# Layer norm scalars of a two-block mixer: three small GpSimd operations in one, against four operations planned apart

## The chip, the cores and the metric

The kernel runs on one core of one Trainium2 chip. The metric is the device time of one execution in microseconds (us). A core has five instruction streams that run beside each other and wait for each other by semaphores: PE (TensorE, the matmuls; its weight loads are listed as PEld), DVE (VectorE), ACT (ScalarE), POOL (GpSimd) and SP (SyncE, which only issues transfers here). Each executes its own instructions strictly in order.

## The reference

The input x is 2048 rows of 512 features. Four stages follow each other: mixer A, mixer B, mixer A, mixer B, each on the layer norm of x and added to x. The layer norm is what the change is about:

```python
def _layernorm(x, axis=-1, eps=1e-5):
    m = jnp.mean(x, axis=axis, keepdims=True)
    v = jnp.var(x, axis=axis, keepdims=True)
    return (x - m) / jnp.sqrt(v + eps)
# A: qkv = x @ wqkv; 32 heads of 16, each position attends to itself and to the
#    positions 2, 4, .. 14 before it; softmax; the result @ wo
# B: h = gelu(layernorm(x) @ w1), its four quarters of features shifted by +1, -1, +2, -2
#    rows, @ w2, added to x: x1;  then x1 + gelu(layernorm(x1) @ w3) @ w4, w3 to 1792 features
x = A_x
x = x + _A_ref(_layernorm(x, axis=-1), A_wqkv, A_wo)
x = x + _B_ref(_layernorm(x, axis=-1), B_w1, B_w2, B_w3, B_w4)
# ... and both once more with the same weights
```

## The kernel before

The rows are cut into four blocks of 512, and a block into four tiles of 128 rows (one row per partition). Layer l = 0, 1 and block b = 0 .. 3 make eight units n = 4 l + b. For each unit there are five stages, whose names stand in the texts below:

- p1: layer norm of x, transposed, times wqkv; q, k and v go out to DRAM (`p1_quarters` for the unit 0, `p1_stream` for the others);
- p2: the attention, on DVE: a product of 128x4096 elements, a sum over it, softmax, a second product and three additions, four times per unit (`p2_unit`);
- p3: the attention's result times wo, added to x, layer norm, transposed, times w1, gelu, into h;
- p4: the shifted h times w2, added to the layer norm's value, layer norm again, transposed;
- p5: times w3, gelu, times w4, over 14 chunks of 128 features, added to x. In unit 0 it works on the weights in f32 as they are; for the other units they are split before into a high and a low f16 half by `big_pair`. Most matmuls take three passes over such halves.

A layer norm of one tile runs so: the sum of the row comes from the instruction that made x; `sq_dev` is an ACT Square with bias and an accumulated sum (the variance, unscaled); `power` makes the two scalars per row from these sums; `normed` applies them to the 128x512 tile on ACT, POOL or DVE; then come transposes on PE and copies into f16 halves. `power` is the place of the change. It is called 84 times: for the four tiles of unit 0's p1, for the 16 tiles of p1 in layer 1 (units 4 to 7), for 32 tiles in p3 and for 32 in p4. Its scalars are columns of small tiles named a (p1), b (p3) and c (p4), with a number for the role: a_0 is the sum, a_1 the squares' sum, a_2 the variance with epsilon (`ve`), a_3 the power (`r`), a_4 the shift (`nb`); in b these are b_0, b_1, b_2, b_3 and b_6. `powers` does the same for four columns at once and stays as it is.

Nothing is scheduled while the program runs. Every operation is entered in a graph with its reads and writes and with the engines on which it could run. Two tables then decide: ORDER lists all operations as 4 x its number + the choice of the engine, and this order is kept on each engine; SLOTS gives each logical buffer its place among the buffers of its kind (mm and acc in PSUM; x, w, f, g, nT, h, kv, prod and so on in SBUF). A list of buffers shared in this way means that an operation can wait for a slot too.

All instructions are issued through one wrapper, so the profile gives them all one line, L282 before (L295 after), and they are told apart by the names of their tiles.

Of the kernel before, what the change touches and what calls it, by code (L numbers as in the profile page):

```python
# [268 lines left out]
def tile_mixer(ctx, tc, x_d, wqkv_d, wo_d, w1_d, w2_d, w3_d, w4_d, out_d):  # L269
# [243 lines left out]
    def sq_dev(key, src, tot, ss, i, r, k=None):  # L513

        s, k = slice(i, i + 1), i if k is None else k
        act(key, lambda: A.activation(junk, src(), AF.Square, bias=tot.t[:, k:k + 1], scale=-float(D),
                                      accum_out=ss.t[:, s]), r + [(tot, k)], [(ss, i)])

    def power(key, ss, ve, r, i, c1, c2, tot, c, nb, k=None, j=None):

        s, k, j = slice(i, i + 1), i if k is None else k, i if j is None else j
# [748 lines left out]
```

## Time and profile before

| | |
|---|---|
| runs before (median; lowest, highest) | 1188.43 us (1188.41, 1188.98) |
| the profiled execution, its own time | 1188.87 us |
| its span, first to last instruction | 1187.0 us |
| mean granted clock of TensorE | 0.99 |
| PE busy | 1144.8 us, 96% |
| DVE, ACT, POOL busy | 919.9, 581.8, 389.5 us |
| main DMA queue | 60.3% of 16 engines' span |

A row of the profile by groups gives the engine and operation, what it writes and reads (buffer numbers left out), the shape, how often, then the busy time in us and the mean of one in ns. A row of the timeline starts with the start and the duration in us, and in brackets stands the idle time before it and what ended it. Rows of stages have the window, its length and, for each engine in turn, its busy time and number of instructions.

### The profile page before, as it was taken

Reading aid. Unit: us, or ns where it says so; the run is one execution under the profiler, and the core shown is the slowest. Engines: PE = TensorE matmul, PEld = TensorE weight load, DVE = VectorE, ACT = ScalarE, POOL = GpSimd, SP = SyncE. Lnnn points to the kernel's source line nnn. Section 1 sums busy time; section 2 is a strip of 40 time slices with the busy share of each in tenths; the row PEclk is TensorE's granted clock in tenths of the full one; section 3 lists DMA queues with packets and bytes.
Section 4 is the critical chain, followed back from the end, with each engine's and each line's share of the span. In section 5 each row is a group of like instructions: output and inputs, shape, how many; then the busy total and the mean of one; then the engine's idle time right before and its main releaser. Section 6 shows DMA issues by size and latency. Waiting matters only on the chain.

```text
span 1187.0 us, 15150 instructions
## 1 busy us (share of the span) xinstructions
PE 1144.8 (96%) x5334; PEld 545.3 (46%) x5334; DVE 919.9 (77%) x992; ACT 581.8 (49%) x1044; POOL 389.5 (33%) x486
## 2 busy tenths in 40 slices
PE   9699999999898999999999999999999999999998
PEld 6444444554343444444444444444444444444454
DVE  6989999999987898599965988889848998224122
ACT  7584465333777454353453546465435463342231
POOL 4320021021556514341752345531516153315000
PEclk9999999899999999999999999999999999999999
DMA  6975664557698645965476786884388546414221
GB/s 217 313 259 174 198 195 142 166 168 183 197 310 244 181 121 124 267 192 145 106 194 211 197 183 159 226 199 148 99 201 256 155 114 197 108 62 112 90 92 62
DMA packets 240533, 206.80 MB, mean 174 GB/s; under 512 B 107276, under 2 KB 167940, under 8 KB 240456
## 3 DMA queue, kind: packets, MB, share of 16 engines
q1 hardware_dynamic: 238784, 204.01, 60.3%
q10 hardware_dynamic: 1672, 1.82, 0.5%
q8 instruction: 42, 0.69, 0.2%
q14 instruction: 35, 0.29, 0.1%
HBM read 141.03 MB, written 39.47 MB: 152 GB/s over the span
## 4 chain that ended last, share of the span: by engine, by line
PE 86%; ACT 5%; DMA 4%; DVE 3%; issue 1%; SPq 1%; POOL 0%; ACTq 0%; DVEq 0%
PE mm L282 60%; PE acc L282 26%; DMA w<-in_A_x_dram 1%; DMA w<-in_B_w_dram 1%; ACT junk L282 1%; ACT g L282 1%; SPq L282 1%; DVE L L282 1%; DVE prod L282 1%; DMA xt<-g 1%; DMA kv<-kv 1%; ACT f L282 1%; ACT ev L282 1%; DVE g L282 0%; POOL g L282 0%
## 5 line engine op out<-in xcount | busy, mean ns | idle before, releaser
L282 PE MATMUL mm<-nT,w 128*128 128x512 f16 (+1 forms) x1288 | 306.7, 391 | 5.2 <-DMA w<-w 4.5
L282 PE MATMUL acc<-w,g 128*128 128x512 f16 (+1 forms) x1260 | 307.3, 393 | 1.7 <-POOL g L282 1.7
L282 ACT ACTIVATE mm<-mm,s_w 128x512 f32<-128x512 f32 (+1 forms) x144 | 90.8, 631 | 254.3 <-PE mm L282 254.1
L282 POOL TENSOR_TENSOR g<-f,g 128x512 f16<-128x512 f32 x80 | 121.6, 1528 | 244.8 <-ACT g L282 149.5
L282 PE MATMUL mm<-wq_hl,xt 128*128 128x512 f16 x864 | 196.5, 380 | 3.4 <-ACT ev L282 1.8
L282 PEld LDWEIGHTS <-w 128*128 128x128 f16 x1344 | 124.9, 98 | 146.3 <-issue 5.0
L282 PEld LDWEIGHTS <-g 128*128 128x128 f16 x1272 | 124.3, 98 | 147.5 <-POOL g L282 2.2
L282 PEld LDWEIGHTS <-xt 128*128 128x128 f16 x1008 | 98.6, 98 | 121.8 <-issue 4.6
L282 DVE TENSOR_TENSOR prod<-kv,L 128x4096 f32<-128x4096 f32 x32 | 141.6, 4426 | 0.1
L282 DVE TENSOR_REDUCE L<-prod 128x256 f32<-128x4096 f32 x32 | 141.0, 4408 | 0.1
L282 DVE TENSOR_TENSOR prod<-kv,q 128x4096 f32<-128x4096 f32 x29 | 128.7, 4439 | 4.5 <-DMA q<-kvq_d 3.7
L282 DVE TENSOR_TENSOR prod<-prod 128x2048 f32<-128x2048 f32 x64 | 115.1, 1798 | 0.2
L282 DVE SCALAR_TENSOR_TENSOR g<-mm,c_g,g 128x512 f16<-128x512 f32 x56 | 41.7, 746 | 89.0 <-ACT g L282 87.8
L282 PE MATMUL mm<-w_hl,h 128*128 128x512 f16 x384 | 87.3, 383 | 4.5 <-DVE h L282 3.8
L282 PE MATMUL mm<-nT,w_hl 128*128 128x512 f16 x384 | 87.3, 379 | 1.8 <-ACT nT L282 1.2
L282 PE MATMUL mm<-wo_hl,oT 128*128 128x512 f16 x384 | 85.8, 379 | 0.0
L282 POOL TENSOR_SCALAR b<-b 128x1 f32<-128x1 f32 (+1 forms) x48 | 24.9, 518 | 176.0 <-ACT junk L282 174.2
L282 ACT ACTIVATE g<-mm,c_g 128x512 f16<-128x512 f32 x98 | 67.0, 685 | 2.0
L282 PEld LDWEIGHTS <-oT 128*128 128x128 f16 x426 | 41.7, 98 | 50.2 <-issue 0.8
L282 ACT ACT_TABLE_LOAD x48 | 61.6, 1283 | 4.8 <-issue 2.1
L282 PEld LDWEIGHTS <-h 128*128 128x128 f16 x384 | 37.8, 99 | 51.2 <-ACT f L282 4.2
L282 PEld LDWEIGHTS <-w_hl 128*128 128x128 f16 x384 | 37.4, 98 | 47.6 <-issue 3.0
(210 smaller groups left out, 1278.9 us busy)
## 6 DMA issues: line engine op xcount, KB each, us to landing
w<-w SPq DMA_DIRECT2D x196, 256.0 KB, 2.7
kv<-kvq_d SPq DMA_DIRECT2D x62, 768.0 KB, 5.2
kvq_d<-ev SPq DMA_DIRECT2D x84, 256.0 KB, 2.6
w<-in_B_w_dram SPq DMA_DIRECT2D x56, 256.0 KB, 4.9
w<-g SPq DMA_DIRECT2D x28, 256.0 KB, 4.2
q<-kvq_d SPq DMA_DIRECT2D x28, 256.0 KB, 5.3
w<-in_A_x_dram SPq DMA_DIRECT2D x16, 256.0 KB, 5.8
x<-in_A_x_dram SPq DMA_DIRECT2D x16, 256.0 KB, 5.3
```

What stands on the lines that cost most here:

```text
L282: i = f(*a, **k).ins
```

## The change

`power` was one graph operation of three POOL instructions: scale with epsilon, power of -1/2, mean times power times a constant. Now it is four operations, each placed on its own. Only the power is bound to POOL. The scale with epsilon (`ve`), the constant times the mean (which waits for the sum alone) and its multiplication by the power may be on ACT, POOL or DVE. On ACT the epsilon has to be a tile (`eps`), which POOL sets once for each of two values. The tables ORDER and SLOTS are new as a whole; of the 252 operations besides the powers, 108 are on ACT, 68 on DVE and 76 on POOL. The rest of the program text is unchanged, but the new tables also move other operations among the engines that they allow, and all of them in time.

```diff
 ORDER = [int(k) for k in """
-16 8 12 32 1576 20 1560 41 28 25 44 36 364 52 60 56 372 64 48 92 852 376 70 96 860 72 124 868 76 101 80 876 188 368
+24 1608 28 16 20 1624 32 36 40 8 0 12 4 417 56 148 412 153 48 160 156 104 44 166 420 118 109 170 52 112 172 192 900
...
+    eps_t = {}
+
     def power(key, ss, ve, r, i, c1, c2, tot, c, nb, k=None, j=None):
 
         s, k, j = slice(i, i + 1), i if k is None else k, i if j is None else j
-
-        def fn():
-            G.tensor_scalar(ve.t[:, s], ss.t[:, j:j + 1], c1, c2, ALU.mult, ALU.add)
-            G.tensor_tensor(r.t[:, s], ve.t[:, s], nhalf[:, :1], ALU.pow)
-            G.tensor_scalar(nb.t[:, s], tot.t[:, k:k + 1], r.t[:, s], c, ALU.mult, ALU.mult)
-        gp(key, fn, [(ss, j), (tot, k)], [(ve, i), (r, i), (nb, i)])
+        if c2 not in eps_t:
+            eps_t[c2] = const.tile([P, 1], F32, name=f"eps{len(eps_t)}")
+            G.memset(eps_t[c2], c2)
+        eb = eps_t[c2]
+        v1 = lambda e: (lambda: e.tensor_scalar(ve.t[:, s], ss.t[:, j:j + 1], c1, c2, ALU.mult, ALU.add))
+        act(key, lambda: A.activation(ve.t[:, s], ss.t[:, j:j + 1], AF.Identity, bias=eb, scale=c1),
+            [(ss, j)], [(ve, i)], also=[(POOL, v1(G), None), (DVE, v1(V), None)])
+        gp(key, lambda: G.tensor_tensor(r.t[:, s], ve.t[:, s], nhalf[:, :1], ALU.pow), [(ve, i)], [(r, i)])
+        v2 = lambda e: (lambda: e.tensor_scalar(nb.t[:, s], tot.t[:, k:k + 1], c, None, ALU.mult))
+        act(key, lambda: A.activation(nb.t[:, s], tot.t[:, k:k + 1], AF.Copy, scale=c),
+            [(tot, k)], [(nb, i)], also=[(POOL, v2(G), None), (DVE, v2(V), None)])
+        v3 = lambda e: (lambda: e.tensor_scalar(nb.t[:, s], nb.t[:, s], r.t[:, s], None, ALU.mult))
+        act(key, lambda: A.activation(nb.t[:, s], nb.t[:, s], AF.Copy, scale=r.t[:, s]),
+            [(r, i)], [(nb, i)], also=[(POOL, v3(G), None), (DVE, v3(V), None)])
```

Three places show how the new order moves instructions. The first is the start, on DVE, where the tiles of block 0 of x (w, in f32) get their statistics (mx) and their normalization (f). Before:

```order
L282 BN_STATS mx_251<-w_244 128x6
L282 BN_AGGR mx_252<-mx_251 128x2
L282 BN_STATS mx_251<-w_246 128x6
L282 BN_AGGR mx_256<-mx_251 128x2
L282 TENSOR_SCALAR f_253<-w_244,a_3_153,a_4_156 128x512
```

And after the change, on the same engine:

```order
L295 SCALAR_TENSOR_TENSOR wq_hl,ssq<-nT_249 128x3x128
L295 BN_STATS mx_260<-w_251 128x6
L295 BN_AGGR mx_256<-mx_260 128x2
L295 BN_STATS mx_260<-w_250 128x6
L295 BN_AGGR mx_255<-mx_260 128x2
L295 TENSOR_SCALAR a_4_156<-a_4_156,a_3_153 128x1
L295 TENSOR_SCALAR a_4_156<-mx_255 128x1
L295 TENSOR_SCALAR f_261<-w_251,a_3_153,a_4_156 128x512
```

A square of a quarter of wqkv (nT to wq_hl, with its sum in ssq) stands first now, and two scalar operations of the powers stand ahead of the first normalization.

The second place is p4 of unit 0, where the f tiles are the residual and its normalization, mm the matmul's result, and c the scalars. On POOL, before, an addition into x and three whole powers:

```order
L282 TENSOR_TENSOR x_296<-x_296,f_294 128x512
L282 TENSOR_SCALAR c_2_208<-c_1_205 128x1
L282 TENSOR_TENSOR c_3_211<-c_2_208,nhalf 128x1
L282 TENSOR_SCALAR c_4_214<-c_0_202,c_3_211 128x1
L282 TENSOR_SCALAR c_2_208<-c_1_205 128x1
L282 TENSOR_TENSOR c_3_211<-c_2_208,nhalf 128x1
L282 TENSOR_SCALAR c_4_214<-c_0_202,c_3_211 128x1
```

After, on POOL:

```order
L295 TENSOR_TENSOR x_275<-x_275,f_300 128x512
L295 TENSOR_TENSOR x_273<-x_273,f_257 128x512
L295 TENSOR_TENSOR c_3_211<-c_2_208,nhalf 128x1 x2
L295 TENSOR_SCALAR c_4_214<-c_0_202 128x1
L295 TENSOR_TENSOR c_3_211<-c_2_208,nhalf 128x1
```

A second addition, into x_273, stands ahead of the powers, and of the scalar operations one is left on POOL. On DVE at the same place, before (prod and L are the attention of unit 1):

```order
L282 TENSOR_TENSOR prod_110<-kv_286,q_293 128x4096
L282 SCALAR_TENSOR_TENSOR f_295,c_0_202<-mm_67,s_w_239,f_295 128x512
L282 SCALAR_TENSOR_TENSOR f_294,c_0_202<-mm_65,s_w_239,f_294 128x512
L282 TENSOR_TENSOR x_269<-x_269,f_295 128x512
L282 SCALAR_TENSOR_TENSOR f_259,c_0_202<-mm_69,s_w_239,f_259 128x512
L282 TENSOR_REDUCE L_287<-prod_110 128x32x8
```

And after:

```order
L295 SCALAR_TENSOR_TENSOR f_300,c_0_202<-mm_69,s_w_241,f_300 128x512
L295 TENSOR_TENSOR prod_110<-kv_292,q_299 128x4096
L295 SCALAR_TENSOR_TENSOR f_257,c_0_202<-mm_69,s_w_241,f_257 128x512
L295 SCALAR_TENSOR_TENSOR f_302,c_0_202<-mm_65,s_w_241,f_302 128x512
L295 TENSOR_REDUCE L_293<-prod_110 128x32x8
L295 TENSOR_SCALAR f_261<-f_257,c_3_211,c_4_214 128x512
```

One residual stands ahead of the product now and two behind it, and the normalization of f_257 has come to DVE, behind the sum L. On PE, the stream matmul of twelve passes that stood behind the three w2 matmuls of p4 stands ahead of them.

The third place is DVE between p5 of unit 0 and p3 of unit 1 (prod, L and mx are the attention of unit 2). Before:

```order
L282 TENSOR_REDUCE L_287<-prod_110 128x32x8
L282 TENSOR_REDUCE mx_251<-L_287 128x32
L282 TENSOR_TENSOR prod_110<-kv_265,L_284 128x4096
L282 TENSOR_TENSOR L_287<-L_287,mx_251 128x256
L282 TENSOR_TENSOR prod_110<-prod_110 128x4x512
```

And after:

```order
L295 TENSOR_REDUCE mx_256<-L_293 128x32
L295 SCALAR_TENSOR_TENSOR junk,ss_p_226<-w_276 128x512
L295 TENSOR_TENSOR L_293<-L_293,mx_256 128x256
L295 TENSOR_TENSOR prod_110<-kv_270,L_290 128x4096
L295 TENSOR_REDUCE mx_256<-L_293 128x32
```

The square of a weight chunk (w, its sum in ss_p), which ACT did before, stands ahead of the product now.

More of the change, by code (lines that the diff above doesn't have):

```diff
@@ L44 @@
 ORDER = [int(k) for k in """
[139 rows of a table removed]
[152 rows of a table added]
 """.split()]
 SLOTS = """
-0012301010000020121101212211333101301023100012110264511134502022161111210300214506016454173221210064522054067103111352
-6425105261703110532046521024010354763101110003220020013210000101012101000030101000100010113110000010031013113000001010
-0002212000110021021011100231200000001011301013010110011010111113011010310002101000050120000001220210100015312000000141
-2103011110000121300112011113000101110210110006112000220142020000001331210100014007843001302213021103102001112323121021
@@ L190 @@
-4012542236111710050610233125231442127526070301103014231565230011230111122210122200132060024104130612103023446143521420
-2076134152640154361252204072362114171442054310321001111120201021201211030401202011001000060021002201331210100004200200
-0000117108042000022632100010410402243410410237235310221400625140103703261405420071606412710313416252350602711054211112
-1110152001011051111011022121210210000000210201220121001002201531020122005054622451011112225211022004112350014421230451
-2306204123507233432462261753131323253015255042656045740363215440501012151601210150201000140610313012201220051010000200
@@ L195 @@
-3211201220020010002200330731004123031634531023115513316410150402001230133440513763604231351016132253411035751604000532
-3362050124173160131214150001201012131315150021200000022006212101000061020000200031210102010084561360145302112201121254
-0403202514116301421032231150460013730625225401513231561407201320367155412252163730272551053010234012021044130105233012
-1011302311263620245233702512013530606023240437033612545203712250250245812300023225030001213204021361233421602131126203
-30210615234703210512222100206725215315201430220212117625103433135126212625124033307
+3010210211323020111010000200202300010133110012100025421234513106780001200110320456216554123722630161350024062740105134
@@ new lines @@
+1563115430024721526453613021504360756100200010200110012221001001230001000011113111030013103111100101031001101101001000
+0013212001100031021000000031200100000001321000110100011011330100110011011002100000010120010001020210011013312001110111
+0113110001033120310121020204022130200210001014112001010160021001101031200100006202152110323212130003024220030431200320
+3012403665207105340172333724602635203335420247040406500378362120100141023310234310000503213214141302013224474361622325
+3134205062675335142126145533004155633274165100500201121111301110611303031620112010101100110020000100131200001015101101
@@ new lines @@
+1000121420316114425311530131513011106425203303122312042655000671211315423650500761453205561611411020417630341202500010
+0315160121314003010215052000201100100002202100110140120011101510210011015335872450114156354310135113010453351504360340
+3125323102173004262450034342560265412070240213353250063614000340230212141400212100220200130111211001000110130121010101
+1202000110023121001100012146212025303104521032401105005011002316047213041112533010513616451517103263010324511636325472
+0313022025253110000004100130011041030105122100211120010001100101010110102001101330110110005205830101115204030001131252
@@ L200 @@
+1012432544026726621304202310502245752141063260553123102067032300470263420250154121470520022250023112012130032115233411
+4214620313054072245061120137241562320224742561201032145134132425001356800351016240211001201025130155021221540131705006
+23010020114133105224113731120122102736131715326431327536333031102126224621115036337
 """
```

289 rows, old and new, of the table ORDER are left out of this document.

## The prediction

> **What bounds the kernel now.** I read the page's head and engine shares, then its chain, the stages, and the places where PE stands still.
>
> ```profile
> span 1187.0 us, 15150 instructions
> PE 1144.8 (96%) x5334; PEld 545.3 (46%) x5334; DVE 919.9 (77%) x992; ACT 581.8 (49%) x1044; POOL 389.5 (33%) x486
> PE 86%; ACT 5%; DMA 4%; DVE 3%; issue 1%; SPq 1%; POOL 0%; ACTq 0%; DVEq 0%
> 60.00:290.00 230.00, 219.96 (x921) 110.14 (x920) 223.81 (x200) 114.62 (x210) 31.02 (x61) 0.98 0.61 185
> 320.00:380.00 60.00, 53.94 (x242) 23.77 (x241) 47.65 (x78) 43.48 (x83) 36.03 (x37) 0.97 0.93 275
> 400.00:1150.00 750.00, 746.02 (x3549) 341.48 (x3548) 548.36 (x584) 344.68 (x580) 271.81 (x311) 1.00 0.59 160
> ```
>
> The stage rows give the window, its length, the busy time of PE, PE's weight loads, DVE, ACT and POOL, the granted clock, the DMA share and GB/s. PE is the bound: 42 us of the span are not matmul, and from 400 to 1150 only 4. From 60 to 290 DVE is as full as PE (223.81 of 230 us), so lateness on DVE can show there. POOL, the engine that is relieved, has no share of the chain, and two thirds of its time is idle. PE does the same matmuls after the change, so no gain can exceed its 42 us of idling and what the half clock costs; a loss has no such limit. So I look only at the places where PE waits in the first 400 us.
>
> **The split itself.** In one power before, at the program's start, the lines show POOL's three operations:
>
> ```profile
> 5.66 0.18 DVE L282 BATCH_NORM_AGGREGATE mx<-mx 128x2 f32<-128x6 f32 x1
> 5.93 0.19 POOL L282 TENSOR_SCALAR a<-mx 128x1 f32<-128x1 f32 x1 [1.58 <-DVE mx L282]
> 6.21 0.57 POOL L282 TENSOR_TENSOR a<-a,nhalf 128x1 f32<-128x1 f32 x1
> 6.88 0.27 POOL L282 TENSOR_SCALAR a<-mx,a 128x1 f32<-128x1 f32 x1
> 7.19 0.55 DVE L282 TENSOR_SCALAR f<-w,a,a 128x512 f32<-128x512 f32 x1
> L282 ACT ACTIVATION_READ_ACCUMULATOR wq_hl<-nT 128x1 f32 x4 | 0.8, 190 | 0.0
> L282 ACT ACTIVATE kv<-mm 128x128 f32<-128x128 f32 x3 | 0.8, 269 | 0.1
> L282 DVE TENSOR_SCALAR inv_w<-inv_w 128x1 f32<-128x1 f32 x2 | 0.3, 154 | 0.1
> ```
>
> The chain takes 6.88 + 0.27 - 5.93 = 1.22 us, and the normalization follows 0.04 us later. No 128x1 ACTIVATE exists before; its cost lies between the 190 ns of the accumulator's read and the 269 ns of an ACTIVATE of 128 columns. I take 230 ns, the middle. After the change the chain is scale-and-epsilon 0.23, power 0.57, times-the-power 0.23 and two hand-overs of about 0.09 us, the gap from DVE's aggregate (5.66 + 0.18) to POOL's 5.93: 1.21 us. Alone it is no shorter and no longer, within 0.1 us. In load, ACT gets 108 of the 252 scalar operations, 108 x 0.23 = 25 us (20 to 29); DVE gets 68, 68 x 0.154 = 10.5 us; POOL loses 176 small ones. ACT is idle half the time: nothing for that. 15 of the 84 powers stand before p4(1), so 15/84 x 10.5 = 1.9 us of DVE's addition falls in the stage where DVE is full.
>
> The Trainium skill (ScalarE: Activation LUTs, What ACT_TABLE_LOAD costs) speaks against the change: an ACTIVATE pays 186 ns and 93 ns more for each pointer operand, so each chained operation on ACT would take about 280 ns, an estimate from that page. No row here has that shape; by it the chain would be 1.31 us, 0.1 longer than mine, and the sum 0.1 to 0.2 us higher.
>
> **Start, 0 to 64 us: 0.** The order now puts all four transposes of block 0 before the first qkv matmul, and on DVE a square of weights before the first statistics. Walking the new order with the durations of before, that matmul starts near 14.9 us instead of 9.13. It is swallowed later:
>
> ```profile
> 54.62 0.58 PE L282 MATMUL mm<-ss_w,ones 128*128 128x1 f32 x2 [4.32 <-ACT w_hl L282]
> 57.98 0.58 PE L282 MATMUL mm<-ss_wo,ones 128*128 128x1 f32 x2 [2.77 <-ACT wo_hl L282]
> 62.98 1.46 PE L282 MATMUL mm<-wq_hl,xt 128*128 128x512 f16 x3
> 54.00:64.00 10.00, 5.06 (x18) 3.47 (x19) 9.97 (x20) 9.94 (x21) 3.55 (x6) 0.51 1.05 396
> 39.33 4.42 DVE L282 TENSOR_TENSOR prod<-kv,x 128x4096 f32<-128x4096 f32 x1
> ```
>
> PE waits 7.1 us there for squares of weights on ACT, and by my walk the first stream matmul stays at 62.95 against 62.98. The matmuls of 54 to 64 run at half clock (0.51); with a shorter wait before them up to half of their 5.06 us, 2.5, may come back, but only if they end the stage, and the weight squares do. Two of the four first loads of wqkv and the pads of kvq go from SP's queue to ACT's, ahead of ACT's first table load, when ACT has only these weights to wait for: 0 too. DVE, however, begins its first product at about 41.6 instead of 39.33, 2.3 us late. I cost that at nothing, because p3(0) has PE work from the streams queued ahead of it; without this cover it goes to the slower rival.
>
> **p4(0), 195 to 212 us: +1.1.** Here PE waits for layer-norm powers, and the place is visible whole:
>
> ```profile
> 195.90 4.41 DVE L282 TENSOR_TENSOR prod<-kv,q 128x4096 f32<-128x4096 f32 x1
> 202.84 4.41 DVE L282 TENSOR_REDUCE L<-prod 128x256 f32<-128x4096 f32 x1
> 201.80 1.59 POOL L282 TENSOR_TENSOR x<-x,f 128x512 f32<-128x512 f32 x1 [39.31 <-DVE f L282]
> 203.47 0.19 POOL L282 TENSOR_SCALAR c<-c 128x1 f32<-128x1 f32 x1
> 206.97 0.27 POOL L282 TENSOR_SCALAR c<-c,c 128x1 f32<-128x1 f32 x1
> 201.81 2.75 PE L282 MATMUL mm<-wq_hl,xt 128*128 128x512 f16 x12
> 204.40 0.60 PE L282 MATMUL mm<-ident,o 128*128 128x128 f32 x4
> 206.62 0.66 PE L282 MATMUL mm<-ident,f 128*128 128x128 f32 x4 [1.62 <-ACT f L282]
> 208.71 1.97 PE L282 MATMUL mm<-ident,f 128*128 128x128 f32 x8 [1.44 <-ACT f L282]
> 211.37 5.10 PE L282 MATMUL mm<-nT,w 128*128 128x384 f32 x10 [0.69 <-ACT nT L282]
> 204.00:212.00 8.00, 4.26 (x20) 3.05 (x19) 8.00 (x8) 6.13 (x10) 2.60 (x8) 0.74 0.18 57
> ```
>
> Before, POOL does one add and three powers from 203.47 to 207.24, while PE fills 2.6 us of it with a stream matmul; the up-projection starts at 211.37. In the new order that stream matmul (2.75 us) stands ahead of the three w2 matmuls instead, so the last w2 matmul ends near 204.6 and only the 0.6 us transposes are left as cover. DVE does the first residual and then the 4.41 us product, so the third tile's residual, f_257, ends near 205.4; then POOL must add x_273 with it (about 1.6 us, in order, to 207.0) before the first power. Three powers follow to about 209.2. But the end is DVE's: the normalization f_261 moved from ACT to DVE behind the 4.41 us reduce (206.2 to 210.6). It ends at 211.1; transposes 0.7 and ACT's copy 0.6 give 212.45: 1.1 us later. From below, had the add not stood ahead, the powers would end at 207.6, but f_261 would hold the end all the same unless the reduce came later; from above, 1.1 plus DVE's 1.9. I take 1.1. PE's gap is then 3.8 us instead of 1.62, 1.44 and 0.69; the clock (0.74 here) is halved in both.
>
> **p3(1) to p4(1), 290 to 320 us: +1.3.**
>
> ```profile
> 298.66 0.69 DVE L282 SCALAR_TENSOR_TENSOR x<-acc,x 128x512 f32<-128x512 f32 x1 [0.72 <-PE acc L282]
> 308.71 0.88 DVE L282 SCALAR_TENSOR_TENSOR h<-mm,c_h,h 128x384 f16<-128x384 f32 x2 [1.64 <-ACT h L282]
> 293.19 0.63 ACT L282 ACTIVATE junk<-w 128x512 bf16<-128x512 f32 x1 [3.19 <-DMA w<-in_B_w_dram]
> 289.73 4.42 DVE L282 TENSOR_TENSOR prod<-kv,L 128x4096 f32<-128x4096 f32 x1
> 316.01 1.65 DVE L282 SCALAR_TENSOR_TENSOR h<-mm,c_h,h 128x384 f16<-128x384 f32 x4
> 317.80 4.05 PE L282 MATMUL mm<-w_hl,h 128*128 128x512 f16 x12 [3.75 <-DVE h L282]
> PE mm L282 <- DMA w<-w: 4.5, 3, 2.4
> ```
>
> The square of 293.19 moves from ACT to DVE, ahead of the product that DVE started at 289.73. Its DMA lands at 293.2, so DVE idles 3.5 us in front of it. Part comes back, as DVE waited 0.72 and 1.64 us later on; DVE's order to the last low half of h ends near 319.1 instead of 317.66, and PE's 317.80 becomes about 319.1. The 1.1 of p4(0) is mostly inside this idling (DVE would wait for the same DMA). I add half of it: 0.5.
>
> **320 to 1187.** Before, PE loses 6.1 us from 320 to 380, 4.5 of it in three waits for loads of w (the last row above: total, times, longest). DMA is 93% busy, and the change moves no bytes. I let it be, as with the last 37 us. From 400 PE is full; the normalizations have their slack.
>
> Sum: 0 + 1.1 + 1.3 + 0.5 = 2.9 us on the span of 1187.0. The profiled run took 1188.87, 1.87 more than its span and 0.44 over the median 1188.43, so the prediction is 1188.43 + 2.9 = 1191.3 us.
>
> **Rivals.** (a) Faster, 1182. With ACT's part of one power beside POOL's part of another, three powers take 3 x 0.66 instead of 3.77 us at p4(0): 1.8 less; if the gap stays short, the 26% of the clock lost over those 8 us comes back, 2.1; with the 2.5 at the start, 6.4. For it: the three powers were serial there. Against it: the adds ahead and the reduce. Locks speak for it too:
>
> ```profile
> 347.13 4.36 POOL L282 TENSOR_SCALAR c<-c,c 128x1 f32<-128x1 f32 x1
> 346.94 4.42 DVE L282 TENSOR_TENSOR prod<-kv,q 128x4096 f32<-128x4096 f32 x1
> ```
>
> An operation of 0.27 us takes 4.36, until DVE's two-input product ends. Most such cases stand after 400, where PE is full, so they give nothing. The Trainium skill (SBUF — State Buffer, SBUF: two separate sides) has this as an exclusive port lock held for a whole instruction; the trace agrees with 4.36 against 4.42 us.
>
> (b) No change, 1188.5: the waits for w at 365 to 378, ended by transfers and not by PE, take up the 2.9 us. For it the 93%; against it, that a load may only start when PE frees its buffer.
>
> (c) Slower, 1195: the cover of the start is gone, and DVE carries 2.3 + 1.9 = 4.2 us of lateness to the last h of p3(1), on top of the sum less its half term: 2.4 + 4.2 = 6.6. It decides if DVE's first reduce after p3(0) starts over 3 us late; the 97% of DVE's stage speaks for it, the idle 6.2 us of it against.
>
> Chances: forecast 0.34, (a) 0.25, (b) 0.26, (c) 0.15. The measurement tells about 0.2%, 2.4 us, from no change: faster is (a), 0.25; the same is (b) and a fifth of the forecast's, 0.33; slower is the rest, 0.42. The forecast's own range is 1189 to 1194. The range reaches from 1 us below (a) to (c) with DVE's 4.2 us counted once more, 1181 to 1200; that leaves out the tails of both.
>
> **What will show it.** Right: the first stream matmul within 0.5 us of 63; a gap of more than 3 us ahead of the p4(0) transposes and the up-projection at 212 to 213; PE's first p4(1) matmul at 319 to 320; 128x1 ACTIVATE rows at 0.19 to 0.28 us; 400 to 1150 with no more than 6 us idle. Wrong: the up-projection before 211, p4(1) over 322, or PE gaps after 400 where a power stands behind a POOL tile or an ACT operation that waits.

## The result: 1.0% slower, lost in the first 25 us

| | before | after the change |
|---|---|---|
| median of 4 runs each | 1188.70 us (1188.41 to 1189.56) | 1200.38 us (1198.80 to 1204.95) |
| ratio, 95% interval | | 1.0103 [1.0075, 1.0131] |
| the profiled execution | 1188.87 us, span 1187.0 | 1200.44 us, span 1198.6 |

The forecast was 2.9 us and its range ended at 1200; the change cost 11.7 us. The head of the profile after, the engine shares and the chain:

```profile
span 1198.6 us, 15185 instructions
PE 1149.3 (96%) x5334; PEld 547.5 (46%) x5334; DVE 924.0 (77%) x1052; ACT 599.8 (50%) x1145; POOL 381.6 (32%) x409
PE 76%; DVE 7%; DMA 6%; ACT 5%; issue 2%; POOL 2%; SPq 1%; ACTq 0%; DVEq 0%; POOLq 0%
```

PE is as full as before, 96%, with 4.5 us more of busy time, and the other shares hardly move. Only the chain says that something happened: PE's share of it fell from 86 to 76%, and DVE, DMA and POOL took eight of the ten points. To find where, I count a lag from the matmul rows of both traces: each matmul counts by one duration of its shape (the warm matmuls on the tile of ones are left out), and the lag at a time t is how much later the changed kernel has done as much of this work as the kernel before had done at t.

| t, us | 25 | 62 | 200 | 220 | 320 | 340 | 380 | 450 | 550 | 860 | 990 | end |
|---|---|---|---|---|---|---|---|---|---|---|---|---|
| lag, us | +9.3 | +10.3 | +7.5 | +11.6 | +10.1 | +10.3 | +6.7 | +6.7 | +10.2 | +9.2 | +11.6 | +11.6 |

9.3 of the 11.6 us are there after 25 us. The stages of the start, before (first three rows), and then after, with two later stages that are used further down (the columns are window, length, then PE, weight loads, DVE, ACT, POOL, granted clock, DMA share, GB/s):

```profile
0.00:25.00 25.00, 23.09 (x123) 17.38 (x124) 15.72 (x39) 16.94 (x42) 12.57 (x37) 1.00 0.81 258
25.00:50.00 25.00, 23.76 (x134) 15.43 (x132) 22.18 (x31) 12.05 (x37) 8.67 (x7) 1.00 0.69 223
50.00:75.00 25.00, 16.36 (x70) 8.37 (x69) 23.30 (x39) 23.83 (x55) 8.18 (x11) 0.80 0.96 350
```

```profile
0.00:25.00 25.00, 17.82 (x82) 13.04 (x83) 12.68 (x33) 11.13 (x24) 7.05 (x30) 0.80 0.83 268
25.00:50.00 25.00, 25.00 (x128) 17.27 (x127) 19.90 (x38) 13.76 (x38) 8.79 (x7) 1.00 0.33 100
50.00:75.00 25.00, 14.33 (x73) 8.33 (x72) 22.76 (x27) 17.05 (x45) 10.57 (x11) 0.80 0.99 350
340.00:380.00 40.00, 38.03 (x179) 17.30 (x177) 34.35 (x65) 31.21 (x74) 24.43 (x25) 1.00 1.05 284
400.00:1150.00 750.00, 741.95 (x3504) 338.32 (x3503) 552.48 (x630) 356.74 (x643) 261.73 (x253) 1.00 0.59 160
```

In the first 25 us PE is busy 5.3 us less and gets only 0.80 of its clock. From 25 to 50 PE stands still nowhere, but the DMA engines move at a share of 0.33 instead of 0.69: (0.69 - 0.33) x 25 = 9.0 us of transfers that were done by then before are not done now. From 50 to 75 the transfers are full in both kernels, so nothing of that can be caught up there.

ACT's first 10 us, in the timeline before (three rows) and after (the ACTq rows are transfers that ACT issues):

```profile
0.71 1.34 ACTq L282 DMA_DIRECT2D nT<-in_A_wqkv_dram  x2
2.08 1.28 ACT L282 ACT_TABLE_LOAD   x1 [2.08 <-issue]
3.82 0.52 ACT L282 ACTIVATE wq_hl<-nT 128x384 bf16<-128x384 f32 x1 [0.46 <-DMA nT<-in_A_wqkv_dram]
```

```profile
0.73 2.95 ACTq L295 DMA_DIRECT2D nT<-in_A_wqkv_dram  x4
4.36 2.56 ACTq L295 DMA_DIRECT2D kvq_d<-prod  x2
6.96 1.28 ACT L295 ACT_TABLE_LOAD   x1 [6.96 <-DVE mx L295]
8.25 0.52 ACT L295 ACTIVATE wq_hl<-nT 128x384 bf16<-128x384 f32 x1
8.78 0.19 ACT L295 ACTIVATE a<-mx 128x1 f32<-128x1 f32 x1
```

Six issues instead of two hold ACT's own instructions back until 6.96 us: the two pads alone run from 4.36 to 6.92. (The profile names DVE's mx as what ended this wait, but ACT is issuing up to 6.92.) ACT's first useful instruction comes 4.4 us later than before, and the second thing it does is the constant times the mean of the first power, which POOL did before. DVE's shift and normalization, and PE, wait behind it (the last row is the kernel before's):

```profile
9.07 0.21 DVE L295 TENSOR_SCALAR a<-a,a 128x1 f32<-128x1 f32 x1 [1.76 <-ACT a L295]
9.32 0.55 DVE L295 TENSOR_SCALAR f<-w,a,a 128x512 f32<-128x512 f32 x1
10.02 0.63 PE L295 MATMUL mm<-ident,f 128*128 128x128 f32 x4 [2.49 <-DVE f L295]
15.04 0.58 PE L295 MATMUL mm<-g,minus_id 128*128 128x512 f16 x1 [1.41 <-ACT g L295]
18.71 3.63 PE L295 MATMUL mm<-nT,oT 128*128 128x256 f32 x8
...
9.13 1.99 PE L282 MATMUL mm<-nT,oT 128*128 128x256 f32 x8 [0.69 <-ACT oT L282]
```

So the first transposes start 2.2 us later (7.81 before), then the four tiles' transposes and corrections follow each other with waits between them, and the first qkv matmul comes at 18.71 instead of 9.13. What that does to the rest of the start is seen on SP's queue (SPq), after and then before:

```profile
17.35 0.42 SPq L295 DMA_DIRECT2D nT<-in_A_wo_dram  x1
39.12 0.33 SPq L295 DMA_DIRECT2D kvq_d<-kv  x1
49.08 0.64 SPq L295 DMA_DIRECT2D w<-in_A_x_dram  x1
```

```profile
30.79 0.82 SPq L282 DMA_DIRECT2D kvq_d<-x  x2
38.46 0.61 SPq L282 DMA_DIRECT2D w<-in_A_x_dram  x1
```

After 17.77 SP issues nothing until 39.12, 21.4 us; before, its pause was from 18.49 to 30.79, 12.3 us. The next entry in its order is the store of k and v, which by the profile waits for copies of PE's results by DVE (5.2 us) and ACT (16.3 us), and the loads of block 1 of x and of the small weights stand behind it. The first load of x comes at 49.08 instead of 38.46. PE's waits at the end of the start are then no shorter than before, only later: from 25 to 75 us PE is idle for 10.7 us, before for 9.9 (PE, after):

```profile
58.63 2.11 PE L295 MATMUL acc<-wq_hl,g 128*128 128x384 f16 x12 [2.37 <-ACT x L295]
64.45 0.59 PE L295 MATMUL mm<-ss_w,ones 128*128 128x1 f32 x2 [3.70 <-ACT w_hl L295]
69.37 1.54 PE L295 MATMUL mm<-ident,f 128*128 128x128 f32 x6 [4.34 <-POOL f L295]
```

The first stream matmul follows at 72.41, where before it was 62.98: 9.4 us of lag have come through.

p4(0) of the changed kernel, on PE, DVE and POOL:

```profile
216.37 0.66 PE L295 MATMUL mm<-ident,f 128*128 128x128 f32 x4 [3.85 <-ACT f L295]
219.20 1.94 PE L295 MATMUL mm<-ident,f 128*128 128x128 f32 x8 [2.18 <-DVE oT L295]
221.83 6.54 PE L295 MATMUL mm<-nT,w 128*128 128x384 f32 x11 [0.69 <-ACT nT L295]
...
207.85 4.42 DVE L295 TENSOR_TENSOR prod<-kv,q 128x4096 f32<-128x4096 f32 x1
213.53 4.41 DVE L295 TENSOR_REDUCE L<-prod 128x256 f32<-128x4096 f32 x1
217.86 0.53 DVE L295 TENSOR_SCALAR f<-f,c,c 128x512 f32<-128x512 f32 x1
...
208.08 6.54 POOL L295 TENSOR_TENSOR x<-x,f 128x512 f32<-128x512 f32 x2 [34.97 <-DVE f L295]
```

And p4(1), one row of the list of PE's waits (total, times, longest), and the 128x1 operations on ACT by shape:

```profile
327.95 5.28 PE L295 MATMUL mm<-w_hl,h 128*128 128x512 f16 x12 [3.70 <-DVE h L295]
PE mm L295 <- DMA w<-w: 3.0, 3, 1.3
L295 ACT ACTIVATE c<-c,eps 128x1 f32<-128x1 f32 x21 | 5.9, 288 | 0.3
L295 ACT ACTIVATE b<-b,b 128x1 f32<-128x1 f32 x23 | 6.7, 291 | 19.3 <-POOL b L295 19.3
```

### The profile page after: what moved, and what is told of

It is laid out like the page before. It is cut to its first block, busy times and chain, and to the rows that moved or that the text cites. A ratio compares the mean times of both kernels' runs of the same rounds, so it can differ in the third digit from the quotient of the medians.

```text
span 1198.6 us, 15185 instructions
## 1 busy us (share of the span) xinstructions
PE 1149.3 (96%) x5334; PEld 547.5 (46%) x5334; DVE 924.0 (77%) x1052; ACT 599.8 (50%) x1145; POOL 381.6 (32%) x409
## 4 chain that ended last, share of the span: by engine, by line
PE 76%; DVE 7%; DMA 6%; ACT 5%; issue 2%; POOL 2%; SPq 1%; ACTq 0%; DVEq 0%; POOLq 0%
PE mm L295 53%; PE acc L295 23%; DMA kvq_d<-ev 3%; DVE prod L295 2%; DVE L L295 2%; POOL g L295 1%; SPq L295 1%; ACT ev L295 1%; ACT L295 1%; DMA w<-w 1%; ACT f L295 1%; DMA nT<-g 1%; ACT g L295 1%; DMA w<-g 1%; DMA nT<-in_A_wo_dram 1%
## 5 line engine op out<-in xcount | busy, mean ns | idle before, releaser
L295 POOL TENSOR_TENSOR g<-f,g 128x512 f16<-128x512 f32 x83 | 141.0, 1703 | 260.1 <-ACT f L295 123.8
L295 DVE TENSOR_TENSOR prod<-prod 128x2048 f32<-128x2048 f32 x64 | 118.6, 1853 | 0.1
L295 POOL TENSOR_SCALAR b<-b 128x1 f32<-128x1 f32 (+1 forms) x43 | 17.2, 400 | 145.6 <-DVE x L295 92.8
L295 PEld LDWEIGHTS <-h 128*128 128x128 f16 x384 | 37.9, 99 | 50.8 <-ACT a L295 4.2
```

What stands on the lines that cost most here:

```text
L295: i = f(*a, **k).ins
```

## The experiments

They are told in the order of their questions. An edit that moves operations in the order may need another buffer table as well. The versions that only place the scalars elsewhere, move the pads or add warm matmuls keep their table as it is; of the 1617 buffers, p4(0) put back and the later corrections move one, and where it is more, the number is given. A diff shows the edit to the tables in words where numbers would tell nothing. Ratios are to the kernel before, run on the same chip. The lags of all of them stand in a table at the end.

**Is it the split, the engines or the order?** Each power as four operations of its own, but all on POOL and in the place of the old one:

```diff
 # tables of before
-power: POOL (scale with eps, power, mean x power)
+ve: POOL   nbc: POOL   power: POOL   nbr: POOL
```

> The order and the buffers of before, and every power as the four operations of the change, all four on POOL and where the one operation stood. 'The order costs it': the time is lost by the new order, 9 us of it in the first 20 us, so this stays with before, 1188 to 1190 us; the fourth small operation adds about 0.3 us per power on POOL and PE hides it. 'The split costs it': four operations with a hand-over each are themselves slower, and this is 1194 us or more.

0.9977 [0.9965, 0.9989], 1186.79 us. The split costs nothing and gains 2.6 us; it is the fastest version of this study. In its trace the gap that the kernel before has at 983 is gone (PE before, and in this kernel):

```profile
983.41 2.33 PE L282 MATMUL acc<-w,g 128*128 128x512 f16 x10 [1.73 <-POOL g L282]
...
975.84 7.93 PE L296 MATMUL acc<-w,g 128*128 128x512 f16 x36
```

The same place in the order, with the three scalar operations on ACT:

```diff
 # tables of before
-power: POOL (scale with eps, power, mean x power)
+ve: ACT   nbc: ACT   power: POOL   nbr: ACT
```

> The order and the buffers of before, with the scale, the constant and the last product of every power on ACT, at the place of the old operation, so that ACT waits for POOL's power each time. 'The order costs it': 1188 to 1194 us, the waits on ACT being about 0.7 us each and hidden under PE except at the start and in p4 of unit 0. 'The hand-overs between ACT and POOL cost it': 1197 us or more, as slow as the change.

1.0258 [1.0212, 1.0304], 1220.12 us, more than either theory allowed. ACT's list of waits points to the reason: it now stands still 62 us for POOL's powers in c and b, in order, with its copies out of PSUM queued behind.

```profile
ACT c L296 <- POOL c L296: 32.7, 32, 4.5
ACT b L296 <- POOL b L296: 29.6, 32, 3.8
```

The other way round, the change's order with every scalar operation on POOL:

```diff
 # tables of the change
-252 operations: 108 ACT, 68 DVE, 76 POOL
+252 operations: POOL
```

> The order and the buffers of the change, with all scalar operations of the powers put back on POOL, at their places in the order. 'The order costs it': still 1196 to 1202 us, and the first qkv matmul still later than 16 us. 'The scalars on ACT and DVE cost it': back to 1188 to 1193 us.

1.0314 [1.0288, 1.0339], 1227.30 us. ACT's normalizations wait for POOL instead (f for c and for b, the same list):

```profile
ACT f L296 <- POOL c L296: 37.3, 14, 10.2
ACT f L296 <- POOL b L296: 29.5, 14, 6.1
```

So within its own order, the change's placing on ACT and DVE is worth about 26 us (37.9 over the kernel before, against 11.7), while in the order of before the placing on ACT costs over 30; in both cases the order fits the placing that it was made with. The lag at 25 us is +7.2 here too, so the start isn't lost by the scalars' engines alone.

**Which stretch costs it?** The first 25 us in the order of before (powers split, on POOL), then the change's order:

```diff
-ORDER = order of the change
+ORDER = order of before to 25 us, then the change's order of all the rest
```

> The operations that PE had begun in the first 25 us of before stand first, in the order of before (their powers on POOL); all others follow in the order of the change. 54 of 1617 buffers get another place. 'The start costs it': 9 us are lost in the first 20 us of the change and stay lost, so this is 1190 to 1194 us. 'The start is absorbed', as the prediction had it: the waits for weights at 56 to 70 us end where they end, and this is 1198 to 1202 us.

1.0005 [0.9994, 1.0017], 1190.13 us (10 runs). It is 0.8 us over the before of its own chip, the change 11.7 (the intervals are 1.4 and 3.3 us to each side): the first 25 us carry 10.9 of the 11.7 us. The 54 buffers with another place are part of the edit. In its trace p4(0) still loses 4.2 us (lag 0.8 at 200, 5.0 at 220), and at 380 the lag is -0.3. The loss of p4(0) is real, and at 380 it is made up; by what, is looked at in the section after the experiments.

The order of before up to p4(0), once with buffers as near the change's as could be, once with those of before:

```diff
+ORDER = order of before to 225 us, then the change's
+SLOTS = preferring the change's places   (first)   /   those of before to 225 us (second)
```

> The order of before (powers as four operations on POOL) up to PE's first up-projections of p5 of unit 0 at 225 us, then the order of the change; 110 of 1617 buffers get another place. 'What p4 of unit 0 loses is lost for good': 3 to 4 us under the run with only the start of before, 1185 to 1187 us. 'The waits for w at 365 to 378 us take it up': as that run, 1189 to 1191 us.

> The order of before up to 225 us as in the earlier run, but with the buffers of before for all that begins there; the order of the change behind. 'The buffer table cost that run its 14 us at 62 to 140 us': no loss before 225 us, and 1185 to 1190 us. 'The mix of orders costs it': 1197 us or more again.

1.0090 [1.0073, 1.0107] and 1.0013 [1.0000, 1.0026]: the same order, 9 us apart (1200.74 and 1191.04, or 11.5 and 2.3 over their own before; 306 buffers differ between them). The second has p4(0) in the order of before too and ends no better than the version with the start alone (2.3 against 0.8 us, with 280 buffers at another place than in the change), so nothing of p4(0)'s loss is seen at the end. The first loses 13.1 us between 62 and 140, where its order is that of before. So a table of buffers has a price of its own. To see how large, the tables of the first experiment with nothing but other buffers, legal too:

```diff
 # order and engines of the first experiment
-SLOTS = those of before
+SLOTS = another legal assignment
```

> The order of before throughout (powers as four operations on POOL) with another legal buffer table: the change's places where they are free in this order, the least recently used place elsewhere. 'The buffer table alone makes waits': 10 us or more over the same order with its own table, 1197 us or more. 'Any table that is legal serves': 1187 to 1190 us.

1.0349 [1.0334, 1.0365], 1230.37 us: 43.6 us over the first experiment, with the same operations in the same order on each engine and 1146 buffers at another place. So an experiment here that moves many buffers may carry some of this too; those that keep the table don't.

p4(0) of the version with the start of before put back by hand: the stream matmul of twelve passes behind the three w2 matmuls again, the second add on POOL behind the powers, the normalization of the third tile on ACT.

```diff
 # start of before, then the change's order; at p4(0):
-PE: wq_hl,xt x12; w_hl,h x36; transposes
+PE: w_hl,h x36; wq_hl,xt x12; transposes
```

> The run with the start of before, and p4 of unit 0 put back: the stream matmul behind the three w2 matmuls, the addition into x behind the powers, the third normalization on ACT. 'What p4 of unit 0 loses is lost for good': up-projection 2 to 4 us earlier and 1186 to 1188 us. 'The waits for w at 365 to 378 us take it up': the gain is seen at 220 us and gone at 400, and the time stays at 1189 to 1191 us.

1.0045 [1.0031, 1.0059], 1194.31 us, slower than without the repair. The stream matmul had covered something else where it stood:

```profile
197.44 7.94 PE L296 MATMUL mm<-w_hl,h 128*128 128x512 f16 x36 [2.56 <-DVE h L296]
```

The w2 matmuls now wait 2.56 us for h from DVE. Lag +7.0 at 220, +1.0 at 380: again 4.2 us are made up between 340 and 380; later 4.3 us are lost again without a cause that I could name. As the lag at 220 is no smaller than without the repair (+5.0), this run does not tell what p4(0)'s loss costs.

**What in the start?** The two pads moved from ACT's queue to SP's, behind the loads of w:

```diff
-24 1608 28 16 20 1624 32 36 40 8 0 12 4 417
+24 1608 28 16 20 1624 32 36 40 8 12 417
...
-236 232 432 429 1020 96 248
+236 232 432 429 1020 5 1 96 248
```

> The change with one edit: the two pad transfers (kvq_d from zeros) go from ACT's queue back to SP's, behind the first loads of w. 'ACT's queue makes the start late': ACT's table load begins near 3.7 instead of 6.96 us, the first transpose of x near 8.3 instead of 10.02 us, the first qkv matmul 2 us earlier or more, and the run 1194 to 1198 us. 'The scalars of the first powers make it late': no difference, 1198 to 1202 us.

The scalars of the four first powers on POOL:

```diff
-first four powers: ve, nbc, nbr on POOL, ACT and DVE
+first four powers: ve, nbc, nbr on POOL
```

> The change with one edit: the scalar operations of the first four powers run on POOL instead of ACT and DVE, at their places in the order; the pads stay on ACT's queue. 'The scalars of the first powers make it late': f no longer waits for ACT's operation behind the pads, the first transpose comes near 8.3 us and the run at 1194 to 1198 us. 'ACT's queue is it, with the squares and copies on ACT': 1198 to 1202 us, since the copies of the transposes still wait on ACT.

Both:

> Both edits of the start together. 'ACT's queue and the scalars are the whole of the start's loss': 1189 to 1192 us, as with the start of before. 'PE's own order is the rest (four transposes and their corrections ahead of the first qkv matmul, at half clock)': the first qkv matmul still after 14 us, and 1193 to 1197 us.

| | ratio | median, us | first transposes | first qkv matmul | lag at 25 |
|---|---|---|---|---|---|
| the change | 1.0103 [1.0075, 1.0131] | 1200.38 | 10.02 | 18.71 | +9.3 |
| pads to SP | 1.0050 [1.0035, 1.0065] | 1195.50 | 8.54 | 17.99 | +8.2 |
| scalars to POOL | 1.0071 [1.0056, 1.0086] | 1198.47 | 8.48 | 17.38 | +6.6 |
| both | 1.0064 [1.0047, 1.0080] | 1198.33 | 8.62 | 16.62 | +6.2 |

Each edit alone takes ACT out of the way of the first transposes: they come 1.5 us earlier, and no earlier with both. At 25 us the two are worth 1.1 and 2.7 us, together 3.1. So ACT's queue is a cause, for a third of the lag, by one execution of each version. With the pads gone ACT's table load starts at 3.71 us, but its first square then waits for its load of wqkv until 6.78: of the 4.4 us by which ACT started later, the pads are 1.5. The ends don't follow these lags: the pads alone end 3 us ahead of the two others, with more lag at 25. (The runs of the last one lie between 1190.41 and 1199.39; its profiled execution is the fastest, so its lag at the end stands for that run alone.)

The rest of the order of the start, with both edits in: the third tile's place exchanged with the first's, and the qkv matmuls begun after the first tile.

```diff
 # both edits, and:
-PE: transposes of 4 tiles; qkv
+PE: transposes of tile 1; qkv of it; transposes of tile 2; ...
```

> Both edits of the start (pads on SP, the first four powers' scalars on POOL), and tiles 0 and 2 of block 0 change places in the order up to their transposes, so that tile 0, which the first qkv matmul needs, is loaded, normalized and transposed first and not last; the first two tiles' qkv matmuls come directly behind their corrections. 'The order of the tiles on PE is the rest of the start's loss': the first qkv matmul before 12 us, at most 2.5 us behind before at 30 us, and 1189 to 1193 us. 'The rest sits in what SP sends later': still 5 us or more behind at 70 us, and 1195 us or more.

1.0100 [1.0079, 1.0121], with another place for 43 buffers. The first qkv matmul does come at 11.06 and the lag at 15 us is 2.9, but at 25 it is 5.9 again and the end is no better: PE runs into the next tiles' waits instead. Putting only the f16 corrections of the last two tiles behind the first qkv matmuls:

```diff
 # both edits, and:
-PE: transposes and corrections of 4 tiles; qkv
+PE: transposes of 4 tiles, corrections of 2; qkv; corrections of 2
```

> The run with both edits of the start (pads on SP, first scalars on POOL), and the corrections of the last two tiles (tiles 3 and 0, the matmuls with minus_id that wait for ACT's copy) behind the first qkv matmuls instead of ahead of them. 'PE's waits for ACT's copies are the rest': first qkv matmul 1 to 2 us earlier than 16.6, 4 us behind at 25 us instead of 6.2, 1192 to 1196 us. 'They are not': within 1 us of that run at 25 us.

1.0082 [1.0059, 1.0104], first qkv 16.61, lag at 25 +8.5: no gain, and that first group of 16 matmuls took 5.49 us at half clock.

Is it the transfers? The 22 transfers of the start, with their queues, exchanged between the two orders: the change's transfers in the version with the start of before, and the reverse.

```diff
+engines: start of before   transfers of the start: the change's   (first)
+engines: the change        transfers of the start: those of before (second)
```

> The run with the start of before, but the 22 transfers of that start in the order and on the queues of the change (four weight loads and the pads on ACT, tile 0 of x last). 'The transfers make the start late': PE 5 us or more behind at 25 us and 1195 us or more. 'The order on the engines does': PE at most 3 us behind at 25 us, 1189 to 1193 us.

> The change, with those 22 transfers in the order and on the queues of before, all else as in the change. 'The transfers make the start late': PE at most 4 us behind at 25 us, 1190 to 1194 us. 'The order on the engines does': 7 us or more behind at 25 us, and 1196 us or more, since the engines still take tile 0 last.

1.0073 [1.0056, 1.0091] and 1.0141 [1.0111, 1.0170], with 60 and 49 buffers at another place; both lose the start, by 6.8 and 11.2 us at 25. PE's first transposes in the two:

```profile
12.07 0.85 PE L296 MATMUL mm<-ident,f 128*128 128x128 f32 x4 [4.52 <-DVE f L296]
...
11.75 1.09 PE L296 MATMUL mm<-ident,f 128*128 128x128 f32 x4 [5.09 <-POOL a L296]
```

Each of the two orders of the engines does worse with the other's loads; "it is the queues" and "it is the engines" are both true and cannot be added.

**Is it the half clock?** Warm matmuls up to the first transposes, in the change and in the version with both edits:

```diff
-WARM = 38
+WARM = 62   (the change)   /   WARM = 52   (both edits)
```

> The change with 62 instead of 38 matmuls on ones at the start, so that PE has work until the first transpose at 10 us; the 24 more matmuls compute nothing that is used. 'The half clock is a third of the start's loss': clock 0.9 or more from 10 to 25 us, PE 6 us instead of 9.2 behind at 25 us, and 1196 to 1198 us. 'The half clock only falls into waits': 9 us behind at 25 us as before, 1199 to 1202 us.

> The run with both edits of the start, with 52 instead of 38 matmuls on ones. 'The half clock is a third': 4 us instead of 6.2 behind at 25 us and 2 us under that run's median, 1194 to 1197 us. 'It only falls into waits': no change at 25 us, 1197 to 1200 us.

1.0144 [1.0121, 1.0166] and 1.0100 [1.0069, 1.0132], 8.4 and 6.7 us behind at 25. The clock didn't stay up. Windows of the change, then of the change with 62 warm matmuls:

```profile
10.00:15.00 5.00, 2.12 (x9) 1.32 (x10) 2.70 (x8) 2.88 (x6) 2.07 (x5) 0.73 1.06 376
15.00:20.00 5.00, 4.22 (x13) 2.88 (x13) 3.87 (x7) 3.72 (x9) 0.00 (x0) 0.50 1.14 324
20.00:25.00 5.00, 5.00 (x23) 4.10 (x22) 2.28 (x6) 2.03 (x5) 0.00 (x0) 0.74 0.43 152
```

```profile
10.00:15.00 5.00, 1.69 (x10) 0.97 (x10) 3.10 (x9) 3.21 (x8) 2.06 (x5) 0.90 1.06 382
15.00:20.00 5.00, 4.26 (x14) 2.94 (x14) 3.87 (x7) 3.73 (x9) 0.00 (x0) 0.50 1.14 328
```

It fell to 0.50 from 15 to 20 all the same, so the price of the half clock wasn't isolated. By the records of the change, from 10 to 25 us, it is up to 2.12 x 0.27 + 4.22 x 0.50 + 5.00 x 0.26 = 4.0 us (busy time of each window by the share of the clock that is missing). It isn't the only cause: the version with the tiles exchanged had the full clock up to 25 us and still lags by 5.9.

All lags together; each row is one execution. Those of the split on ACT, the start of before, both, and the start of before with the change's transfers are the fastest of their version, 7.1, 3.2, 7.9 and 3.0 us under its median, so a few us between the ends of two rows say nothing.

| lag, us, at | 25 | 62 | 140 | 200 | 220 | 340 | 380 | 550 | end |
|---|---|---|---|---|---|---|---|---|---|
| the change | 9.3 | 10.3 | 8.9 | 7.5 | 11.6 | 10.3 | 6.7 | 10.2 | 11.6 |
| split, POOL | 0.1 | 0.9 | 1.4 | 1.7 | 1.9 | 1.4 | 0.6 | 0.6 | -2.0 |
| split, ACT | 1.1 | 1.0 | 1.0 | 3.4 | 6.9 | 10.6 | 11.0 | 13.3 | 23.8 |
| change's order, POOL | 7.2 | 8.5 | 6.4 | 10.1 | 15.9 | 14.1 | 13.7 | 21.3 | 38.6 |
| start of before | -0.4 | 2.2 | 2.2 | 0.8 | 5.0 | 3.8 | -0.3 | 0.5 | -1.8 |
| and p4(0) put back | -0.5 | 3.5 | 2.2 | 3.4 | 7.0 | 5.2 | 1.0 | 4.4 | 5.3 |
| before to 225, change's buffers | -0.2 | 1.1 | 14.2 | 15.0 | 13.2 | 14.0 | 9.1 | 12.0 | 11.3 |
| before to 225, its own buffers | -0.2 | 0.2 | 1.9 | 1.9 | 2.6 | 4.6 | 1.2 | 4.4 | 3.0 |
| split, POOL, other buffers | 0.4 | 1.1 | 16.2 | 17.0 | 15.2 | 21.5 | 28.8 | 29.9 | 41.2 |
| pads to SP | 8.2 | 9.3 | 9.4 | 8.0 | 11.1 | 9.1 | 4.5 | 5.7 | 9.0 |
| scalars to POOL | 6.6 | 9.0 | 7.5 | 6.2 | 8.9 | 9.3 | 5.8 | 9.0 | 9.4 |
| both | 6.2 | 7.1 | 6.7 | 5.3 | 8.4 | 6.3 | 1.6 | 2.7 | 1.7 |
| both, tiles exchanged | 5.9 | 7.1 | 7.5 | 6.1 | 9.7 | 10.4 | 6.5 | 9.4 | 10.3 |
| both, corrections later | 8.5 | 10.3 | 9.3 | 7.9 | 11.7 | 10.0 | 5.9 | 7.8 | 9.0 |
| start of before, change's transfers | 6.8 | 9.9 | 8.5 | 7.1 | 11.4 | 10.3 | 5.7 | 9.4 | 7.1 |
| the change, transfers of before | 11.2 | 13.5 | 13.7 | 12.3 | 16.5 | 15.6 | 12.7 | 15.9 | 21.4 |
| the change, 62 warm | 8.4 | 9.4 | 9.7 | 8.4 | 11.1 | 11.7 | 8.0 | 11.3 | 11.2 |
| both, 52 warm | 6.7 | 9.1 | 8.9 | 7.5 | 11.6 | 10.6 | 6.6 | 9.5 | 9.5 |

## Why the prediction was wrong, step by step

**"Start, 0 to 64 us: 0" is the step that failed.** It measured +9.3 us at 25 us, and putting back that stretch alone takes away 10.9 of the 11.7 us. Three parts of it were wrong:

- "Two of the four first loads of wqkv and the pads of kvq go from SP's queue to ACT's ... 0 too." I asked what ACT's weight squares would lose and not what else ACT now does first, nor when its first square's own load comes. ACT's first ACTIVATE comes 4.4 us later, and the first normalization needs one of ACT's scalars, an operation that the change itself put there. Taking the pads away moved the first transposes by 1.5 us, as did taking the scalars away. This is the part of the change that I priced at nothing with a reason that looked at one consumer only.
- "that matmul starts near 14.9 us": it was 18.71. My walk had neither ACT's 6.96 us nor the waits of 1.17 and 1.41 us between the corrections, nor a fallen clock in 10 to 25 us; I looked for the half clock only at 54 to 64.
- "It is swallowed later" by 7.1 us of waits for weight squares. This is where the reasoning failed, not only the size. Those waits end with loads, and the loads stand on SP's queue behind a store that needs PE's results: the first load of x went from 38.46 to 49.08. DVE's first product, which I put at 41.6, started at 47.04. A wait can swallow lateness only if what ends it does not itself wait for what is late. That the lag goes straight through 25 to 62 us is measured; that SP's order is the reason is read from the queue's rows, and no run moved that store alone.

**"p4(0) +1.1"** measured +3.0 to the up-projection: lag 7.5 at 200, and 221.83 - 211.37 = 10.5 there. The mechanism was right up to DVE's normalization. With the lag of 7.5 my 205.4 for the residual f_257 gives 212.9 (it ended at 212.19 + 0.74 = 212.9), and the normalization f on DVE, forecast to end at 211.1 + 7.5 = 218.6, ended at 217.86 + 0.53 = 218.4. What I missed comes after it: the transposes wait, by the profile, for a copy of oT on DVE (to 219.1), and eight of them were left, 1.94 us, where I counted four, 0.7. I had one gap of 3.8 in place of PE's three; the first is 3.85, but the two others stayed, 2.18 and 0.69, so the gaps grew from 3.75 to 6.72 us in all, which is the 3.0. The term was 1.9 us too small, and that is not what the end shows: the version with the start of before has the same loss and ends 0.8 us over its before.

**"p3(1) to p4(1): +1.3", and 0.5 on top,** measured -0.3: p4(1) starts at 327.95, 10.15 after 317.80, the up-projection was 10.5 late. PE's wait there is 3.70, before 3.75; the idling of DVE that I added did not come: DVE idles 0.22 us ahead of the moved square (at 302.65), not 3.5.

**"320 to 1187: let it be"** measured -3.6 from 340 to 380 and +4.9 from there to the end. The first part is where rival (b) looked. PE waited 3.0 us instead of 4.5 for loads of w, and the twelve matmuls behind the first of these waits took 2.75 us instead of 4.44 (the granted clock of 340 to 380 was 0.96 before and 1.00 after): 1.5 + 1.7 us of the 3.6. PE before, and PE's waits for w in the version with the split on ACT, which has the order of before:

```profile
368.19 4.44 PE L282 MATMUL mm<-nT,w 128*128 128x512 f16 x12 [2.39 <-DMA w<-w]
PE mm L296 <- DMA w<-w: 4.2, 3, 2.6
```

But the waits do not take up lateness, as (b) has it. That version comes to 340 with a lag of 10.6 us, waits 4.2 us for w, nearly as before, and leaves 380 with 11.0. In the change and the thirteen versions that have its order and its placing after 225 us, the lag shrinks by 2.9 to 4.9 us, whether it is 3.8 at 340 or 15.6. And the last of the three waits ends at 384.27 in the change, 6.7 us later than before (377.53): these loads come later too. So what p4(0) lost is made up by a gain that comes with the new order; that the two are about equal is luck, and no run isolates what gains there. With the change's order and all scalars on POOL only 0.4 us come back. The second part is 8.0 us of PE idling in 750 where I allowed 6, in small gaps (the longest 1.9) for which I have no one cause. Those fourteen versions all lose there (+0.8 to +3.7 us from 380 to 550), so the rest of the loss stays open.

**"The split itself"** was right as a whole: 0 was forecast, and on POOL it gains 2.6 us. A 128x1 ACTIVATE with a tile as bias or scale takes 286 to 300 ns here, not my 230 (one with neither 187 to 194). The Trainium skill (ScalarE: Activation LUTs, What ACT_TABLE_LOAD costs) had about 280 ns for it, and the trace agrees. But what ACT scalars cost is not their length: 62 us of waits of an in-order engine, where the order wasn't made for them.

**The rivals.** (b), no change, is answered above. (a), faster, fell with a p4(0) that got longer and a start that lost clock instead of winning it. (c), slower, named the start as the place, yet by DVE's lateness up to p3(1); but the lag falls by 2.8 us from 62 to 200 and by 1.5 from 220 to 320, so it wasn't that. What stays open within the start: of the 9.3 us, 3.1 hang on pads and scalars; the other 6 lie in the orders of loads and engines and the clock together, which the exchanges show to be coupled.

## What to carry to other kernels

At the start of a program, write down for each engine what its first instruction now waits for, transfers that it issues itself included, and price a moved DMA issue by everything that stands behind it on that queue. Before saying that a later wait swallows a loss, follow what ends that wait back to its cause: slack absorbs only if its end is independent of the late work, and neither the loads of x behind SP's store nor the loads of w at 365 to 385 were. And a statically ordered kernel is tuned as a whole: the order of the start, the placing on engines and the buffer table each moved the end by 0.8 to 3.7% when one was exchanged without the others, so read a local gain in such a kernel by the end time only.

## What the hardware showed that I had not expected

- Issuing transfers takes an engine's time: on ACT four loads took 2.95 us, 0.64 to 0.89 each, and two pads 1.26 and 0.69 us with a wait of 0.6 between them, before the table load could start (6.96 us; 3.71 without the pads).
- The clock fell to 0.50 though no gap of PE up to there was longer than 2.49 us, and with 62 warm matmuls none was longer than 1.41 us. From 10 to 15 us PE was busy for 2.12 of 5 us in the change and for 1.69 with 62 warm matmuls; with 3.43 of 5 (the tiles exchanged) the clock stayed at 1.00. That window holds 16 qkv matmuls there and transposes and corrections alone in the two others, so the busy share and the kind of work are not told apart. The Trainium skill (TensorE: Matmul & The Clock Gate, Why this matters for your kernels) warns of idle gaps over about 3 us; in these runs shorter ones, many in a row, went with a fall.
- Another legal buffer table, with every engine's order kept, cost 43.6 us, 3.7% of the fastest version.
